# Lightning attention followed by a tanh-shrink MLP: causal scores and outputs in halves of 64 keys, and the attention pieces placed anew

## The chip, the cores and the metric

The kernel runs on one core of one Trainium2 chip. The metric is the device time of one execution in microseconds (us); lower is better. The engines are TensorE (PE; its weight loads are listed as PEld), VectorE (DVE), ScalarE (ACT), GpSimd (POOL) and SyncE (SP). SP and GpSimd issue most of the DMAs.

## What is computed

```python
def _attn_ref(q, k, v, lam):                 # 4 batches, 8 heads, 768 positions, 64 channels
    ...
    for b in range(nb):                      # blocks of 64 positions
        intra = np.einsum('bhic,bhjc->bhij', qb, kb) * Dmask[None]     # lam ** (i - j) for i >= j
        intra = np.einsum('bhij,bhjd->bhid', intra, vb)
        inter = np.einsum('bhid,bhde->bhie', qb * lam_pow[None], kv_state)
        out[:, :, sl] = intra + inter
        kv_state = lam_block[None, :, None, None] * kv_state + np.einsum('bhsd,bhse->bhde', kb * rev_pow, vb)

def _moe_ref(x, w_in, w_out):                # x: 3072 x 512, w_in: 512 x 2048, w_out: 2048 x 512
    h = x @ w_in
    return (h - np.tanh(h)) @ w_out
```

All data are float32 on the chip; the weights arrive as 64-bit floats and are rounded on the chip.

## The kernel before

The sequence is cut into 6 groups of 128 positions (`BLK`); a group with its 4 batches gives 512 token rows. One batch of one group is a *chunk* (g, b): 128 positions, 8 heads as 4 pairs p of 2 (j). Two chunks, (0, 1) or (2, 3), are a *half* of a group.

Dense part. Both matrix products use a Strassen-like scheme of seven products (A and B factors, `FACT`): `up` makes the hidden columns (line 458), tanh is taken on ScalarE (L466) and subtracted on VectorE, and `down`, `down_twice` and `inner_steps` (L640, L693, L542) make the output, some of them with a second level of seven products of 128x128 pieces. Weight pieces (`wb`, 256 KB) come from DRAM by GpSimd's DMA queue through a ring of seven buffers. Group 0 is worked otherwise: `up_plain` (L748) runs while the weights are still being rounded on ScalarE and VectorE (L289 to L296), and `down_first` (L778) while VectorE makes the factor sums (L787 among them).

Attention of group g + 1 runs inside the dense work of group g. For one half it has four pieces:

- `att_transpose` (L323): q and k with channels on partitions. For groups 0 and 1 by TensorE (L336), for later groups by loading 32x32 blocks (32 small DMAs for a chunk, on SP's queue, L143) and a VectorE transpose (L331). q times powers of lambda is made here as well (`qd`, L342).
- `att_scores` (L345): for each head a matmul with 64 rows (channels) by 128 keys, 128 queries moving; the two heads of a pair lie in different row halves of TensorE. VectorE multiplies the result by the decay mask (L356).
- `att_out` (L384): the state read (L400; 64x64 weights, four tiles of TensorE in turn), and the value product with all 128 keys (L406; 128x64 weights), both summed in two PSUM banks, which ScalarE copies to `xt` (L410).
- `att_state` (L363): k is multiplied by its decay (L361), the products of k and v (L374), then on VectorE the state times its decay (L379) plus the product (L380).

`attention(g)` returns these pieces, and the main loop (L887 to L939) places them by hand: the first half's transposes and scores after u = 2 and u = 3 of the up part, its output and state after the second down product; the second half's between the later ones. For group 1 the table `turns` (L846) does so. Each engine executes its own queue in order; the order of each queue is made from program order by a scheduler, except where `tied` or `keep_in_program_order` holds an operation to its place. PSUM has eight banks: `att` four, `ya`, `yb`, `z`, `w` one each.

SP's queue carries the loads of q, k, v (`load_natural`, L131: one DMA of 256 KB per chunk and tensor), the blocks (L143) and the input weights.

The functions that the change touches follow, with the line numbers of the profile.

Of the kernel before, what the change touches and what calls it, by code (L numbers as in the profile page):

```python
# [18 lines left out]
BLK = 128  # L19
# [5 lines left out]
def kernel(  # L25
# [69 lines left out]
    mask = const.tile([128, 2, NP, BLK], F32)  # L95
    for j in range(2):
        for p in range(NP):
            h = 2 * p + j
            nc.vector.tensor_tensor_scan(out=mask[:, j, p, :], data0=lam_all[:, h:h + 1].to_broadcast([128, BLK]),
                                         data1=ident, initial=0.0, op0=AL.mult, op1=AL.add)  # L100

# [13 lines left out]
    bwd = mask.rearrange("s j p i -> s p j i")[:, :, :, BLK - 1:BLK].to_broadcast([128, NP, 2, D])  # L115
# [11 lines left out]
    def load_natural(g, b, names):  # L127
        for name, src, bufs in (("q", q, 2), ("k", k, 3), ("v", v, 4)):
            if name in names:
                x = (qpool if name == "q" else io).tile([128, H, D], F32, name=f"{name}_nat", tag=name, bufs=bufs)  # L130
                op = nc.sync.dma_start(out=x, in_=src[b, :, ts(g, BLK), :].rearrange("h s d -> s h d"))  # L131
                tc.keep_in_program_order(op)
                raw[g, b][name] = x
# [189 lines left out]
    def att_transpose(g, bs):  # L323
        for b in bs:
# [4 lines left out]
            for dst, x in ((qt, "q"), (kt, "k")):  # L329
# [3 lines left out]
                else:  # L333
                    tp = bank("tp", "att", 4).rearrange("d (p s) -> d p s", p=NP)
                    for p in range(NP):
                        tied(g == 0 or p == 0, nc.tensor.transpose(out=tp[:, p, :], in_=t[x][:, 2 * p:2 * p + 2, :],  # L336
                                                                   identity=ident))
                    tied(g == 0, nc.scalar.activation(dst, tp, AF.Copy))
            qd = None
            if g > 0:  # L340
                qd = work.tile([128, NP, BLK], F32, name="qd", tag="qd")
                nc.vector.tensor_tensor(qd, qt, fwd, op=AL.mult)  # L342
            tr[g, b] = (qt, kt, qd)

    def att_scores(g, bs):  # L345
        for b in bs:
            qt, kt, _ = tr[g, b]

            sp = [bank("sp", "att", 4).rearrange("s (p i) -> s p i", p=NP) for _ in range(2)]
            for p in range(NP):  # L350
                for j in range(2):
                    tied(g == 0, nc.tensor.matmul(out=sp[j][:, p, :], lhsT=kt[ts(j, 64), p, :],  # L352
                                                  rhs=qt[ts(j, 64), p, :], start=True, stop=True))
            ss = work.tile([128, 2, NP, BLK], F32, name="ss", tag="ss")
            for j in range(2):
                tied(g == 0, nc.vector.tensor_tensor(ss[:, j], sp[j], mask[:, j], op=AL.mult))  # L356
            sc[g, b] = ss

    def att_decay(g, b):
        kp = raw[g, b]["k"].rearrange("s (p j) d -> s p j d", j=2)  # L360
        tied(g != 1, nc.vector.tensor_tensor(kp, kp, bwd, op=AL.mult))  # L361

    def att_state(g, bs):  # L363
        if g == NG - 1:
            return

        kv = bank("kv", "att", 4).rearrange("d (b p e) -> d b p e", b=2, p=NP)
        for n, b in enumerate(bs):
            kd, vn = raw[g, b]["k"], raw[g, b]["v"]
            if g > 0:  # L370
                att_decay(g, b)
            for p in range(NP):
                for j in range(2):
                    tied(g == 0, nc.tensor.matmul(out=kv[ts(j, 64), n, p, :], lhsT=kd[:, 2 * p + j, :],  # L374
                                                  rhs=vn[:, 2 * p + j, :], start=n == 0 and p == 0, stop=True,
                                                  skip_group_check=True))
        st = state[:, bs[0]:bs[0] + 2]
        if g > 0:
            nc.vector.tensor_tensor(st, st, lam_blk, op=AL.mult)  # L379
            nc.vector.tensor_tensor(st, st, kv, op=AL.add)  # L380
        else:
            tied(True, nc.scalar.activation(st, kv, AF.Copy))

    def att_out(g, bs):  # L384
        half = bs[0] // 2
# [584 lines left out]
```

## Time and profile before

| what | value |
|---|---|
| runs | 668.13, 667.68 and 666.55 us (median 667.68) |
| span of the profiled execution, the only time of its own that the page has | 665.0 us (the runs shown are 1.6 to 3.1 us longer) |
| TensorE busy | 653.9 us (98%) |
| VectorE busy | 480.1 us (72%) |
| ScalarE busy | 214.7 us (32%) |
| GpSimd busy | 195.8 us (29%) |
| moved | 121.74 MB, mean 183 GB/s |
| granted TensorE clock | 1.00 |

A line of a profile's order of time gives start, length (us), engine, source line, operation, out<-in, shapes and count; a bracket at its end gives the idle time of the engine ahead of it and what ended it. Successive instructions of one group are merged into one line. TensorE's matmuls overlap each other, so the distance between the starts of two groups says what the first one cost, and its listed length is a little longer. A float32 matmul of the program appears as two instructions.

### The profile page before, as it was taken

How to read it: one execution, taken by the hardware profiler on the slowest of the kernel's cores; microseconds unless marked ns; L12 is line 12 of the kernel's file. 1: busy time of each engine (PE TensorE's matmuls, PEld its weight loads, DVE VectorE, ACT ScalarE, POOL GpSimd, SP SyncE). 2: the span in 40 equal slices, each digit the busy share in tenths (PEclk: the TensorE clock that was granted, in tenths of full speed). 3: DMA queues.
4: the chain of work that ended last, by engine and by line, in shares of the span. 5: the costliest groups of instructions: out<-in, count | busy, mean ns of one | idle time of the engine just before them, and what ended most of it. 6: DMA issues, size and time to landing. Idle time of an engine off the chain costs nothing.

```text
span 665.0 us, 13269 instructions
## 1 busy us (share of the span) xinstructions
PE 653.9 (98%) x4992; PEld 594.7 (89%) x4992; DVE 480.1 (72%) x869; ACT 214.7 (32%) x413; POOL 195.8 (29%) x340
## 2 busy tenths in 40 slices
PE   8999999999999999999999999999999999999998
PEld 7788888888888999888999988999988899988897
DVE  4568898997778983579885379987368877357753
ACT  4778923423321112341112342112243112233110
POOL 0001416783112444001435101254301264400250
PEclk9999999999999999999999999999999999999999
DMA  9999936997345979425889543698731687610491
GB/s 216 231 205 263 300 123 215 352 316 219 81 93 145 303 221 276 80 35 135 226 247 277 146 74 73 165 286 255 216 72 38 186 260 258 222 37 1 116 295 64
DMA packets 158958, 121.74 MB, mean 183 GB/s; under 512 B 133872, under 2 KB 135024, under 8 KB 158896
## 3 DMA queue, kind: packets, MB, share of 16 engines
q0 software_dynamic: 26400, 86.27, 40.4%
q1 hardware_dynamic: 132352, 34.64, 25.3%
q8 instruction: 39, 0.64, 0.4%
q14 instruction: 23, 0.19, 0.1%
q10 hardware_dynamic: 144, 0.00, 0.0%
HBM read 100.67 MB, written 20.19 MB: 182 GB/s over the span
## 4 chain that ended last, share of the span: by engine, by line
PE 66%; issue 14%; DMA 8%; SPq 4%; POOL 3%; DVE 3%; ACT 1%; POOLq 0%; DVEq 0%; ACTq 0%
PE y L458 13%; PE y L693 12%; PE zw L693 9%; PE z L458 8%; PE y L542 4%; PE w L640 4%; PE y L640 4%; PE sp L352 2%; PE z L542 2%; DMA raw<-in_moe_w_in_dram 2%; PE h L748 2%; DMA wb<-fine 2%; PE op L406 2%; SPq L131 2%; SPq L143 1%
## 5 line engine op out<-in xcount | busy, mean ns | idle before, releaser
L605 POOL DMA_DIRECT2D wb<-fine x168 | 90.5, 539 | 170.3 <-PE y L693 55.9
L466 ACT ACTIVATE th<-g 128x512 f32<-128x512 f32 x76 | 47.6, 630 | 99.5 <-DVE g L471 34.2
L696 ACT ACTIVATE q<-y 128x128 f32<-128x128 f32 x96 | 26.6, 277 | 149.6 <-PE y L693 148.6
L458 PE MATMUL y<-xt,w 128*128 128x256 f32 x320 | 73.5, 380 | 0.0
L458 PEld LDWEIGHTS y<-xt,w 128*128 128x128 f32 x320 | 59.9, 190 | 8.5 <-ACT g L546 0.9
L467 DVE TENSOR_TENSOR g<-g,th 128x512 f32<-128x512 f32 x76 | 52.1, 689 | 21.1 <-ACT th L466 21.0
L693 PE MATMUL y<-wb,g 128*128 128x128 f32 x456 | 60.6, 278 | 0.0
L748 PE MATMUL h<-xt,w 128*128 128x256 f32 x256 | 58.0, 383 | 2.0 <-DVE w L296 2.0
L748 PEld LDWEIGHTS h<-xt,w 128*128 128x128 f32 x256 | 47.7, 190 | 9.9 <-DVE w L296 2.7
L693 PEld LDWEIGHTS y<-wb,g 128*128 128x128 f32 x456 | 55.1, 192 | 1.3 <-issue 0.3
L608 POOL DMA_DIRECT2D wb<-factors x44 | 23.8, 541 | 96.0 <-PE y L640 64.6
L693 PE MATMUL zw<-wb,g 128*128 128x128 f32 x304 | 40.3, 275 | 0.1
L458 PE MATMUL z<-tt,ws 128*128 128x256 f32 x160 | 38.1, 381 | 0.0
L458 PE MATMUL y<-tt,ws 128*128 128x256 f32 x160 | 37.8, 379 | 0.0
L458 PE MATMUL z<-xt,ws 128*128 128x256 f32 x160 | 37.8, 379 | 0.0
L693 PEld LDWEIGHTS zw<-wb,g 128*128 128x128 f32 x304 | 37.0, 192 | 0.2 <-DVE g L698 0.2
L640 PE MATMUL w<-wb,g 128*128 128x256 f32 x160 | 35.8, 382 | 0.0
L640 PE MATMUL y<-wb,g 128*128 128x256 f32 x160 | 35.3, 379 | 0.0
L356 DVE TENSOR_TENSOR ss<-sp,mask 128x512 f32<-128x512 f32 x48 | 31.1, 684 | 5.8 <-PE sp L352 5.8
L640 PEld LDWEIGHTS y<-wb,g 128*128 128x128 f32 x160 | 30.4, 190 | 4.1
L458 PEld LDWEIGHTS z<-xt,ws 128*128 128x128 f32 x160 | 30.4, 190 | 4.1
L640 PEld LDWEIGHTS w<-wb,g 128*128 128x128 f32 x160 | 30.1, 190 | 4.4
(178 smaller groups left out, 1292.6 us busy)
## 6 DMA issues: line engine op xcount, KB each, us to landing
wb<-fine POOLq DMA_DIRECT2D x168, 256.0 KB, 4.2
wb<-factors POOLq DMA_DIRECT2D x44, 256.0 KB, 4.5
v_nat<-in_v_dram SPq DMA_DIRECT2D x24, 256.0 KB, 5.2
wb<-fine_in POOLq DMA_DIRECT2D x24, 256.0 KB, 4.3
k_nat<-in_k_dram SPq DMA_DIRECT2D x20, 256.0 KB, 5.0
raw<-in_moe_w_out_dram POOLq DMA_DIRECT2D x10, 512.0 KB, 4.9
raw<-in_moe_w_in_dram SPq DMA_DIRECT2D x8, 512.0 KB, 6.0
raw<-in_moe_w_in_dram SPq DMA_DIRECT2D x16, 256.0 KB, 5.6
```

The lines of the kernel that those rows point to most:

```text
L131: op = nc.sync.dma_start(out=x, in_=src[b, :, ts(g, BLK), :].rearrange("h s d -> s h d"))
L356: tied(g == 0, nc.vector.tensor_tensor(ss[:, j], sp[j], mask[:, j], op=AL.mult))
L458: nc.tensor.matmul(out=t[:, m, :], lhsT=wt[:, kt, ts(m, 128)], rhs=x[:, kt, :], start=first and m == 0 and kt == 0, stop=kt == 1, skip_gro ...
L466: nc.scalar.activation(th, src, AF.Tanh)
L467: nc.vector.tensor_tensor(dst(c), src, th, op=AL.subtract)
L542: nc.tensor.matmul(out=dst[:, ts(u, 128)], lhsT=a, rhs=b, start=x in (1, 2, 5) and u == 0, stop=True, skip_group_check=True)
L605: nc.gpsimd.dma_start(out=t.rearrange("p m c -> p (m c)"), in_=fine[TWICE.index(n_), SUB.index(x_)].rearrange("p u c -> p (u c)"))
L608: nc.gpsimd.dma_start(out=t, in_=factors[XAT[FACT[n_][1]]][:, 2 * x_:2 * x_ + 2, :])
L640: nc.tensor.matmul(out=t[:, m, :], lhsT=a[:, u, kt, ts(m, 128)], rhs=wb[:, kt, :], start=first and u == 0 and m == 0 and kt == 0, stop=u = ...
L693: nc.tensor.matmul(out=dst, lhsT=a[:, u, :], rhs=wb[:, ts(u, 128)], start=x in (1, 2) and u == 0, stop=u == NU - 1, skip_group_check=True)
L696: nc.scalar.activation(keep, dst, AF.Copy)
L748: tied(u == 0, nc.tensor.matmul(out=hm[c][:, m, :], lhsT=w1[u][:, i, a, ts(m, 128)], rhs=xt[0, t][:, i, :], start=m == 0 and i == 0, stop= ...
```

## The change

From group 1 on, causality is used in halves of 64 keys (`HF`). Early keys (the first 64 of a chunk) are scored against all 128 queries, late keys only against the last 64. For the upper two pairs the two key halves change places on the partitions, so that four 64x64 tiles of TensorE are in use in turn. Masks are 384 wide for each j and chunk instead of 512. The value product becomes `out_late` (128x64 weights: for the last 64 queries all keys) and `out_early` (64x64 weights: for the first 64 queries the early keys).

- k and v of groups from 1 on are loaded by three DMAs each (128, 64 and 64 rows) instead of one, and k has four buffers instead of three.
- The mask of group 0 lies in the buffer `tt`; `masks()` builds the new one from it with four scans on VectorE and small copies on GpSimd.
- The decay of a chunk's k is two operations of 256 columns, called ahead of the stretch, and `qd` has a call of its own.
- `att_stretch` runs state read, state products, state update and late output; then, where `nxt` is given, the scores of the other half; then the early output. Without `nxt` the first matmul of `out_early` gets a wait on the state's add. With `nxt` the scores also use the banks `ya`, `yb` and `w`, and the state product has the bank `ya` or `yb`.
- Matmuls of attention are all held in program order.
- `pieces` places them anew: in group 2 both halves' stretches stay apart from scores; in groups 1, 3 and 4 the first half's stretch takes in the second half's scores; transposes of groups 4 and 5 start at the end of the dense work of the group before; group 5 has read, late and early output at separate places.

```diff
-    mask = const.tile([128, 2, NP, BLK], F32)
+    HF = BLK // 2
+    mask0 = xpool.tile([128, 3, 2, HB], F32, name="tt", tag="tt").rearrange(
+        "s a b c -> s (a b c)")[:, 0:2 * NP * BLK].rearrange("s (j p i) -> s j p i", j=2, p=NP)
...
+    mask = const.tile([128, 4, 3, HF], F32)
+    def masks():
...
+        for n in range(4):
+            tc.keep_in_program_order(nc.vector.tensor_tensor_scan(
+                out=cross[hi, n].rearrange("s c i -> s (c i)"), data0=lam_all[hi, n + 4:n + 5].to_broadcast([HF, BLK]),
+                data1=inj[hi], initial=0.0, op0=AL.mult, op1=AL.add))
...
-        for name, src, bufs in (("q", q, 2), ("k", k, 3), ("v", v, 4)):
+        for name, src, bufs in (("q", q, 2), ("k", k, 4), ("v", v, 4)):
...
+                    for rows, hs, at_ in ((slice(0, BLK), 0, 0), (slice(0, HF), NP, HF), (slice(HF, BLK), NP, 0)):
+                        n = rows.stop - rows.start
+                        part = src[b, hs:hs + NP, g * BLK + at_:g * BLK + at_ + n, :]
+                        tc.keep_in_program_order(nc.sync.dma_start(out=x[rows, hs:hs + NP], in_=part.rearrange("h s d -> s h d")))
...
+    def score_products(g, b, tags):
+        qt, kt, _ = tr[g, b]
+        sp = [bank("sp", t, 4 if t == "att" else 1)[:, 0:6 * HF].rearrange("s (q c i) -> s q c i", q=2, c=3) for t in tags]
...
+        for late_, rows, cols in ((False, slice(0, BLK), lambda c: slice(0, 1 + c, c)), (True, slice(HF, BLK), None)):
+            for q in range(2):
+                for j in range(2):
+                    for p in (q, q + 2):
+                        c = 1 + p // 2
+                        dst = sp[j][half(p, late_), q, c if late_ else cols(c), :]
+                        tied(True, nc.tensor.matmul(out=dst, lhsT=keys(p, j, late_), rhs=qt[ts(j, 64), p, rows],
+                                                    start=True, stop=True))
...
+    def out_late(g, bs):
...
+                    tied(True, nc.tensor.matmul(out=dst(n, p, j)[:, HF:BLK], lhsT=vn[:, 2 * p + j, :],
+                                                rhs=ss[:, j, p % 2, 1 + p // 2, :], start=False, stop=True,
+                                                skip_group_check=True))
+    def out_early(g, bs, behind=None):
...
+                        r = ts(p // 2, HF)
+                        mm = tied(True, nc.tensor.matmul(out=dst(n, p, j)[:, 0:HF], lhsT=vn[r, 2 * p + j, :],
+                                                         rhs=ss[r, j, q, 0, :], start=False, stop=True,
+                                                         skip_group_check=True))
+                        if behind is not None:
+                            tc.add_manual_dep(mm.ins, behind.ins.name, mybir.DependencyInfo(
+                                mybir.DependencyClass.Sync, mybir.DependencyReason.DATA), reason="state read")
+                            behind = None
+        copy_xt(g, bs[0] // 2, ops)
+    def att_stretch(g, bs, nxt=None, kvtag="att", tags=()):
+        att_read(g, bs)
+        kv = state_products(g, bs, bank("kv", kvtag, 4 if kvtag == "att" else 1))
+        st = state[:, bs[0]:bs[0] + 2]
+        nc.vector.tensor_tensor(st, st, lam_blk, op=AL.mult)
+        add = nc.vector.tensor_tensor(st, st, kv, op=AL.add)
+        out_late(g, bs)
+        if nxt is not None:
+            sp = [score_products(g, b, tags[2 * n:2 * n + 2]) for n, b in enumerate(nxt)]
+        out_early(g, bs, None if nxt is not None else add)
...
-    turns = [(1, 11, 1, ()), (1, 21, 1, ()), (1, 12, 1, ()), (1, 22, 1, ()), (2, 11, 2, p0[0:1]), (2, 21, 2, p0[1:2]),
-             (3, 11, 1, ()), (3, 21, 1, p0[2:4]), (2, 12, 1, ()), (2, 22, 1, p1[0:1]), (3, 12, 1, p1[1:2]),
-             (3, 22, 1, ())]
+    turns = [(1, 11, 1, ()), (1, 21, 1, ()), (1, 12, 1, ()), (1, 22, 1, ()),
+             (2, 11, 2, ((att_transpose, 1, P0), (att_qd, 1, P0))), (2, 21, 2, ((att_scores, 1, P0), (att_decay, 1, P0))),
+             (3, 11, 1, ((att_transpose, 1, (2,)),)),
+             (3, 21, 1, ((att_transpose, 1, (3,)), (att_stretch, 1, P0, P1, "ya", ("att", "att", "yb", "ya")), (att_qd, 1, P1))),
+             (2, 12, 1, ()), (2, 22, 1, ((att_decay, 1, P1),)), (3, 12, 1, ()), (3, 22, 1, ())]
...
+    def pieces(g, at_):
+        h, k = g + 1, g + 2
+        if g == 1:
+            table = {2: [(att_transpose, h, P0)], 3: [(att_scores, h, P0), (att_qd, h, P0), (att_decay, h, P0)],
+                     "P2": [(att_stretch, h, P0)], "P4": [(att_transpose, h, P1)],
+                     "P5": [(att_scores, h, P1), (att_qd, h, P1), (att_decay, h, P1)],
+                     "P6": [(att_stretch, h, P1), (att_sums, h)]}
+        elif g == 2:
+            table = {0: [(att_transpose, h, P0)], 1: [(att_scores, h, P0), (att_qd, h, P0)], 2: [(att_transpose, h, (2,))],
+                     3: [(att_transpose, h, (3,)), (att_decay, h, P0)]}
+        else:
+            table = {1: [(att_transpose, h, P1)], 3: [(att_decay, h, P0)] if h < NG - 1 else []}
+        if 1 < g < NG - 2:
+            table.update({"P2": [(att_stretch, h, P0, P1, "yb", ("att", "att", "w", "yb")), (att_qd, h, P1)],
+                          "P5": [(att_decay, h, P1)], "P6": [(att_stretch, h, P1), (att_sums, h)],
+                          "inner": [(att_transpose, k, P0)], "end": [(att_scores, k, P0), (att_qd, k, P0)]})
+        if g == NG - 2:
+            table.update({"P2": [(att_read, h, P0), (att_scores, h, P1, ("att", "att", "w", "yb"))],
+                          "P4": [(out_late, h, P0), (out_early, h, P0), (att_qd, h, P1)], "P5": [(att_read, h, P1)],
+                          "P6": [(out_late, h, P1), (out_early, h, P1), (att_sums, h)]})
+        run(table.get(at_, ()) if g < NG - 1 else ())
```

In `pieces`, the numbers are the steps u of the up part of group g, and P2 to P6 the places after down products 2, 4, 5 and 6.

## The prediction

> **What bounds the kernel now.** I read the page first, then the clock, TensorE's order of time round one attention stretch, the single instruction starts in it, and VectorE's order of time at the same place.
>
> ```profile
> span 665.0 us, 13269 instructions
> ...
> PE 653.9 (98%) x4992; PEld 594.7 (89%) x4992; DVE 480.1 (72%) x869; ACT 214.7 (32%) x413; POOL 195.8 (29%) x340
> ...
> PEclk9999999999999999999999999999999999999999
> ```
>
> TensorE is busy 98% of the span at full clock. So the time follows the work and the waits on TensorE, and little else. Attention from the second group on is what the change touches; here is one half of group 2 (two chunks), in TensorE's order of time (start, length, line, shapes):
>
> ```profile
> 202.49 2.06 PE L352 MATMUL sp<-qt,kt 64*128 64x128 f32 x32
> 204.47 7.17 PE L640 MATMUL w<-wb,g 128*128 128x256 f32 x32
> 211.57 1.10 PE L400 MATMUL op<-qd,state 64*64 64x128 f32 x32
> 212.61 1.97 PE L406 MATMUL op<-ss,v_nat 128*64 128x128 f32 x32
> 214.41 1.10 PE L374 MATMUL kv<-v_nat,k_nat 128*64 128x64 f32 x32
> 215.44 1.16 PE L693 MATMUL y<-wb,g 128*128 128x128 f32 x8
> ```
>
> Read the starts, not the lengths: scores 1.98 us, read 1.04, output 1.80, state 1.03, then dense work again. With 0.09 at each entry a half costs 2.08 + 3.95 = 6.03 us; the five groups repeat it within 0.01. (A float32 product stands as two instructions.)
>
> **Prices, from single starts in these stretches.** The read puts four 64x64 tiles side by side: starts at 0, 6, 13 and 20 ns, and the next four 109 ns after (128 columns). Scores and output have two tiles side by side, also 109 to 112 ns. The state has two tiles of 64 columns every 58.5 ns. First weights of a mode: 0.05 us for 64 columns. Changing the tile shape: 0.11 (read's last group to output: 0.22 for a slot of 0.11). Back to dense: 0.10 drain, plus 0.10 of dense weights not loaded ahead.
>
> **Unknown price:** four 64x64 tiles with 64 columns. Bounds: 58.5 ns a group (state row) and 109 (read row, as if halving bought nothing). I take 58.5: in the read, the second set of four weight loads starts 55 ns after the first, so four loads side by side keep up with it.
>
> **The matmuls, per half.** Scores become 8 groups of 128 columns (early keys) and 8 of 64 (late): 0.09 + 0.05 + 0.87 + 0.47 + 0.10 = 1.58 us alone, 0.50 less than 2.08. Output becomes 16 pairs of 64 columns (0.94, state row) plus 8 groups (0.47), but with one more change of shape. A stretch of read, state, late, early: 0.09 + 0.92 + 0.11 + 0.99 + 0.94 + 0.16 + 0.47 + 0.10 = 3.77, 0.18 less than 3.95. Merged with the other half's scores (1.34): 5.12 against 6.03, and one dense return less: 1.02 saved.
>
> By the built order of the changed kernel, groups 1, 3 and 4 have one stretch of each kind: 0.50 + 1.02 + 0.18 = 1.69 each. Group 2 keeps its four apart: 1.35. The last (no state; 2 x 5.10 before) runs five pieces, 1.58, 2.45, 1.81, 1.11 and 1.81, with one more return: 1.34. Rows alone: **-7.8 us**.
>
> **What comes back as waits.** The early output of an unmerged stretch now waits for the state add on VectorE; in a merged one the last scores reuse the bank that the add empties. VectorE is in order, and what stands ahead of the add decides. Group 2's first half, before:
>
> ```profile
> 213.47 0.68 DVE L664 TENSOR_TENSOR o<-q,w 128x512 f32<-128x512 f32 x1
> ...
> 215.27 0.68 DVE L379 TENSOR_TENSOR state<-state,fwd 128x512 f32<-128x512 f32 x1
> ...
> 218.28 0.68 DVE L380 TENSOR_TENSOR state<-state,kv 128x512 f32<-128x512 f32 x1
> ```
>
> The add ended 3.5 us after dense work had resumed, and nobody cared. It starts a new piece every 0.60 us there. In the new order I walk from 204.65, the start of the first mask: four masks of 384 elements (0.47 each, about three quarters of 0.60), two sums of 0.60 and eight small ones of 0.20 bring it to 209.4; nine pieces of 0.60, the o above among them, to 214.8; then the state's product, one more sum and the add (0.65, 0.60, 0.70): end at 216.7. The read starts at 211.05 (scores saved 0.5) and the early output could start 3.07 later, at 214.1. **Wait 2.6 us.** Queued behind it on TensorE: all the down product.
>
> At the second half of groups 2, 3 and 4 the five pieces that close the sixth product stand ahead:
>
> ```profile
> 238.84 0.69 DVE L707 TENSOR_TENSOR q<-q,q 128x512 f32<-128x512 f32 x1
> 239.57 1.29 DVE L709 TENSOR_TENSOR q<-q,q 128x512 f32<-128x512 f32 x2
> 240.78 0.69 DVE L379 TENSOR_TENSOR state<-state,fwd 128x512 f32<-128x512 f32 x1
> ```
>
> With the decays gone from before them they start 0.3 earlier; product and add end at 241.9; the early output could start at 238.16 + 3.07 = 241.2. 0.7 each, 2.1 together. The merged stretches of groups 3 and 4: the new order puts the add's end 4.45 us after the read's start, the bank is wanted at 3.8: 0.65 each, 1.3. Sum of these six pieces of waiting: **+6.0**.
>
> **Group 1** runs while weights are still rounded: ScalarE busy 13.3 and VectorE 13.0 of the 14 us from 58 to 72. Two new add waits (about 1.8 and 1.0 by the same walk) stand against filling a weight wait of 0.9 to 1.1 at 67.2 with transposes and dense work moved ahead; later the first down product already waits for VectorE (0.6 and 0.2 on L787). I let 0.5 of its 1.7 survive: **+1.2**. The split loads also fall here: eight more DMAs on SP ahead of weights. Between 0 (SP is already held back by full queues: v took 2.84 where q took 0.58) and 8 x 0.58 = 4.6 us; value 0.
>
> **What goes away:** TensorE waits of 0.3 and 0.9 at 223 to 225, 0.9 at 333 and some 0.6 more from 425 to 545, most of them on wb pieces landing. TensorE arrives later at the first, and the blocks for groups 4 and 5 load earlier, away from the down products. I take 1.5 of 2.7: **-1.5**. Ends: none, and all.
>
> **At nothing:** four scans of 64x128 (0.40 each by L99) and nine small GpSimd pieces at about 36 us, where VectorE is busy 17.3 of 28 us and GpSimd idle until 57; uncovered 1.6 and some 3 us (0.2 to 0.3 each by the identity's rows). Two decays of 256 cost 0.12 more than one of 512, two masks save 0.27. Transposes put earlier: SP then must deliver group 3's first blocks by about 272; from the release at 213 it takes 6 us of natural loads and four blocks of 8 us, 253; if that cover went, VectorE and all behind it would stand. Later SP waits 31 and 29 us for buffers, so its extra 0.5 us issues are covered.
>
> **Sum:** -7.8 + 6.0 + 1.2 - 1.5 = -2.1. On the profiled 665.0 us that is 662.9; the runs shown lie 1.6 to 3.1 above the span (median 667.68), so I forecast **665.6 us**.
>
> **Rivals.**
> - *The waits stay hidden* (0.13). For: part of the work ahead of the add could slip behind it. Against: the new order has it in front. Then -7.8 + 1.2 of group 1 and, as TensorE comes no later to the wb pieces, only 0.6 of relief: -7.2, 660.5.
> - *The saving is only exchanged for waits* (0.15): VectorE, 77.6 of 105 us busy per group, sets each down product's pace, and TensorE's gain returns to it. Only the 0.5 of group 1 stays: 667.2. It is also the case in which halving the keys does not do what it says.
> - *The add comes later still* (0.22), the one on the other side. Place: the eight waits (two each in groups 1 to 4). Price: each 0.1 us of lateness beyond my walk costs 0.8. From 0.26 each the gain is gone; at one more 128x512 piece each (0.60 x 8 = 4.8) the time is 670.4. For it: any VectorE piece that itself waits adds up; against: the walk used measured starts.
> - *Half-width groups cost a full one* (0.09): 160 groups x 50.5 ns = 8.1 us, 673.7; pays back the gain from 71.6 ns a group on. Against: the 55 ns above.
>
> The Trainium skill's "TensorE: Matmul & The Clock Gate", Back-to-back issue gap, gives matmuls of 1 to 64 columns a floor of about 25 ns start to start, so 100 ns for a group of four; by it the last rival's price would be an estimated 6.6 us and the time about 672. The trace speaks against it: tiles side by side start 6 to 7 ns apart. It has 0.03 of that rival's 0.09.
>
> **How the numbers follow.** Forecast case 0.41, its own spread 663 to 668. About 0.2%, 1.3 us, is what a measurement here can tell from no change. The forecast case splits into 0.33 faster, 0.07 same, 0.01 slower; the exchange for waits into 0.01, 0.13, 0.01. Faster: 0.33 + 0.13 + 0.01 = 0.47. Same: 0.07 + 0.13 = 0.20. Slower: 0.01 + 0.01 + 0.22 + 0.09 = 0.33. Range **660.5 to 671.5**: it takes in the first three cases and all but the far end of the add's lateness, and leaves out the half-width rival and a full 4.6 us on SP.
>
> **What would show it.** Right: scores of a half end 1.5 us after their start; state's 32 instructions still 0.94; groups of 64 columns every 58 to 60 ns; TensorE idle before the early output "<-DVE state", 2 to 3 us at the first half of group 2 and 0.5 to 1 at the others; fewer waits on wb. Wrong: groups of 64 columns at 100 ns; no idle there; waits on q_blk or k_blk by VectorE; weights landing later than 53 us in group 1's stage.

## The result, and the profile after

The changed kernel takes 673.91 us (median of 4 runs, 672.60 to 676.93); the kernel before, run beside it, 667.24 us. The ratio is **1.0112, 95% interval 1.008 to 1.0144**: about 1% slower. The forecast was 665.6 us, the range 660.5 to 671.5; a loss had been given a chance of 0.33.

The page of the changed kernel, its span, TensorE's share and clock:

```profile
span 670.3 us, 14720 instructions
...
PE 647.2 (97%) x5632; PEld 588.6 (88%) x5632; DVE 477.3 (71%) x889; ACT 214.5 (32%) x413; POOL 200.8 (30%) x349
...
PEclk9999999999999999999999999999999999999999
```

TensorE's busy time fell by 6.7 us (the rows had forecast 7.8), and the span grew by 5.3: TensorE now stands still for 23 us where it stood for 11. Its waits name what for (engine, line, what it waited for: us in all, times, longest):

```profile
PE op L502 <- DVE state L517: 5.7, 5, 2.5
PE y L800 <- DMA wb<-fine: 2.7, 4, 1.3
...
PE sp L451 <- DVE state L517: 2.2, 3, 1.2
...
PE zw L800 <- DVE ss L458: 1.4, 1, 1.4
```

L502 is the early output, L451 the scores, L517 the state's add, L800 the down products, L458 the masks. The first and third lines are the waits that the forecast had. The other two it had not. The first half of group 2 in TensorE's order, to be read beside the same stretch of before:

```profile
203.15 1.57 PE L451 MATMUL sp<-qt,kt 64*64 64x128 f32 x64
204.65 7.17 PE L747 MATMUL w<-wb,g 128*128 128x256 f32 x32
211.75 1.10 PE L481 MATMUL op<-qd,state 64*64 64x128 f32 x32
212.79 1.15 PE L414 MATMUL kv<-v_nat,k_nat 128*64 128x64 f32 x32
213.77 1.10 PE L490 MATMUL op<-ss,v_nat 128*64 128x64 f32 x32
217.37 0.69 PE L502 MATMUL op<-ss,v_nat 64*64 64x64 f32 x32 [2.49 <-DVE state L517]
```

Scores end 1.50 us after their start, early output takes 0.62; between late and early output lies the wait (bracket: idle time, and what ended it). VectorE at that place, with the o, the state's product and the add that the prediction named:

```profile
213.60 0.68 DVE L771 TENSOR_TENSOR o<-q,w 128x512 f32<-128x512 f32 x1
...
215.43 0.69 DVE L516 TENSOR_TENSOR state<-state,fwd 128x512 f32<-128x512 f32 x1
...
216.63 0.68 DVE L517 TENSOR_TENSOR state<-state,kv 128x512 f32<-128x512 f32 x1
```

VectorE never stops here, and the add simply stands late in its queue: it ends at 217.3, TensorE goes on at 217.37.

**Where the time came from.** I take the start of the same dense product in both traces and follow by how much the changed kernel lags. It lags 0.2 us at 204 us (0.7 without what group 2's first scores save), 2.6 behind group 2's first stretch, 4.2 behind its second, 3.8 where the down products that hold group 3's attention begin, 3.9 at those of group 4, 4.8 at those of group 5, 5.3 at the end. The pieces of TensorE's order, with their waits taken off, give the rows.

| term | forecast | measured | out of |
|---|---|---|---|
| rows, groups 2 to 5 | -6.1 | -5.8 | half scores 1.59 for 2.08; stretch 3.77 for 3.95; merged 5.21 for 6.03; last group behind its first scores 7.19 for 8.12 |
| waits for the add, groups 2 to 4 | +6.0 | +6.7 | 2.56 + 3 x 0.84 + 2 x 0.81 |
| group 1 in all | -0.5 | +0.7 | lag at 204 us |
| masks of the last group | 0 | +1.4 | L458 wait at 545 us |
| wb pieces and all else | -1.5 | +2.3 | what is left of 5.3 |
| sum | -2.1 | +5.3 | spans 665.0 and 670.3 |

The forecast misses the span by 5.3 + 2.1 = 7.4 us: 0.3 on rows, 0.7 on the add's waits, 1.2 in group 1, 1.4 for the masks, 3.8 in the row of wb pieces and all else. Of that row's +2.3, the waits for wb pieces that can be named make +1.6 (at 222 to 240 us 2.8 for 1.4 before; 0.6 at 368 and 0.5 at 443 are new; 0.9 at 333 is gone); the other 0.7 is not placed.

And the profiled execution is one of the better ones: two of the four took 675.2 and 676.9. The median lies 3.6 us above the profiled span, where the forecast had added 2.7. The clock, below, is a part of this.

### The profile page after: what moved, and what is told of

Its sections match the earlier page's. It is cut to its first block, busy times and chain, and to the rows that moved or that the text cites. A ratio compares the mean times of both kernels' runs of the same rounds, so it can differ in the third digit from the quotient of the medians.

```text
span 670.3 us, 14720 instructions
## 1 busy us (share of the span) xinstructions
PE 647.2 (97%) x5632; PEld 588.6 (88%) x5632; DVE 477.3 (71%) x889; ACT 214.5 (32%) x413; POOL 200.8 (30%) x349
## 4 chain that ended last, share of the span: by engine, by line
PE 51%; SPq 19%; DMA 12%; DVE 8%; issue 4%; ACT 4%; POOL 1%; DVEq 0%; ACTq 0%; POOLq 0%
SPq L174 14%; PE y L800 8%; PE acc L889 7%; DMA q_blk<-in_q_dram 6%; PE h L859 6%; PE y L565 6%; PE zw L800 6%; PE z L565 4%; PE w L747 3%; PE y L747 3%; PE y L649 3%; DMA v_nat<-in_v_dram 3%; SPq L163 2%; SPq L158 2%; DVE g L574 2%
## 5 line engine op out<-in xcount | busy, mean ns | idle before, releaser
L800 PE MATMUL y<-wb,g 128*128 128x128 f32 x456 | 60.6, 278 | 1.8 <-DMA wb<-fine 1.8
L800 PEld LDWEIGHTS y<-wb,g 128*128 128x128 f32 x456 | 55.1, 192 | 3.0 <-issue 2.3
L800 PE MATMUL zw<-wb,g 128*128 128x128 f32 x304 | 40.2, 275 | 0.0
L800 PEld LDWEIGHTS zw<-wb,g 128*128 128x128 f32 x304 | 37.0, 192 | 0.0
L565 PEld LDWEIGHTS z<-tt,ws 128*128 128x128 f32 x160 | 29.5, 190 | 5.6 <-DVE g L601 1.8
```

Source lines behind the costliest of these rows:

```text
L565: nc.tensor.matmul(out=t[:, m, :], lhsT=wt[:, kt, ts(m, 128)], rhs=x[:, kt, :], start=first and m == 0 and kt == 0, stop=kt == 1, skip_gro ...
L800: nc.tensor.matmul(out=dst, lhsT=a[:, u, :], rhs=wb[:, ts(u, 128)], start=x in (1, 2) and u == 0, stop=u == NU - 1, skip_group_check=True)
```

## The experiments

All ratios are to the kernel before, run beside the experiment on the same chip. The experiments ran on four chips (e1 to e4, e5 to e8, e9 to e12, e13 and e14), so across these sets the ratios are the better comparison.

| kernel | median us | ratio (95% interval) |
|---|---|---|
| changed | 673.91 | 1.0112 (1.008 to 1.0144) |
| e1_peek | 677.80 | 1.0165 (1.0144 to 1.0186) |
| e2_free_bank | 676.18 | 1.0132 (1.0096 to 1.0168) |
| e3_whole_loads | 679.75 | 1.0186 (1.0161 to 1.0212) |
| e4_old_order | 670.42 | 1.0047 (1.0028 to 1.0066) |
| e5_early_peek | 673.34 | 1.0092 (1.0062 to 1.0121) |
| e6_all | 671.09 | 1.0083 (1.0053 to 1.0114) |
| e7_spread | 674.97 | 1.0124 (1.0104 to 1.0143) |
| e8_from_third | 664.46 | 0.9957 (0.9934 to 0.998) |
| e9_third_spread | 662.40 | 0.992 (0.990 to 0.9939) |
| e10_all_third_spread | 666.60 | 0.9985 (0.9964 to 1.0007) |
| e11_group1 | 674.05 | 1.0099 (1.0075 to 1.0124) |
| e12_keep_busy | 677.79 | 1.0158 (1.0123 to 1.0194) |
| e13_late_transpose | 663.00 | 0.9925 (0.9903 to 0.9948) |
| e14_before_spread | 666.09 | 0.9988 (0.9971 to 1.0004) |

My first theory: the waits for the add are the loss, and what is taken off them comes back, but for a part that wb pieces take. Rival: TensorE's time is only exchanged between waits.

### The add's wait: e1, e2, e5

Read and early output write the same bank from different row halves of TensorE, and the program puts a wait between them. In every kernel with halves here one lies between them (in merged stretches by way of the last scores), so no run shows what happens without it; the add is only what the wait hangs on. So another, cheaper operation to wait for was tried: a copy of one element on ScalarE (`peek`).

```diff
+        look = work.tile([128, 1], F32, name="look", tag="look")
+        peek = nc.scalar.activation(look, kv[:, 0:1, 0, 0], AF.Copy)   # e1, e2: behind the add; e5: ahead of the state's two operations
-        out_early(g, bs, None if nxt is not None else add)
+        out_early(g, bs, None if nxt is not None else peek)            # e1; e5 from group 2 on
+        out_early(g, bs, peek if nxt is not None else add)             # e2
```

> The changed kernel, but in the six stretches that are not merged the first early-output product waits for a one-element copy on ScalarE (it reads the state product's bank) and no longer for the state add on VectorE. Theory (the add waits are real losses of TensorE): the gaps between late and early output, 2.6 us in group 2's first half, 0.8 in the second halves of groups 2 to 4 and 1.0 in group 1, together 6.0 us, shrink to below 0.2 each; wb pieces that land late take up to half of it back, so 668 to 671 against 673.9. Rival (the time is only exchanged: TensorE arrives earlier and waits for wb or VectorE instead): gaps gone, time 673 to 674. Second rival (ScalarE is late itself): gaps stay over 0.5.

e1's edit missed its aim. The copy was written behind the add, reads the same bank, and so waited for the add itself; the gap before the early output was 2.75 us. e2 (state product in bank z, in group 1 in w; the same copy, for the merged stretches) missed in the same way:

> The changed kernel, but the three merged stretches put the state product into a bank of its own (z; in group 1 w) that no score product of the stretch reuses; the early output waits for a one-element copy on ScalarE. Theory: the waits of the last scores for the state add (0.8 us each in groups 3 and 4, 1.2 in group 1) go; 2.9 us less, at least 1.5 of it kept: 671.0 to 672.4. Rival (exchange): 673 to 674.

The waits at the merged stretches of groups 3 and 4 only fell from 0.81 to 0.40, now ahead of the early output. In group 1 a gap of 3.2 us appeared ahead of the last transposes; the trace puts it down to a load of k that landed late, not to the copy. Neither run tells theory and rival apart. What they show is the price of a long gap (below).

> The changed kernel, but in the unmerged stretches of groups 2 to 4 the first early-output product waits for a one-element copy on ScalarE that stands ahead of the state's product and add and so needs the state products alone (in e1_peek the copy came out behind the add, and the wait stayed). Theory (the add waits are real losses): the gaps before the early output in groups 2 to 4 (2.6, 0.8, 0.8, 0.8 us) fall below 0.3, the half-speed stretch of the clock that follows the 2.6 us gap in most executions does not come, wb pieces take up to 2.6 back: 667.5 to 670.5 against 673.9. Rival (exchange for wb waits): 672.5 to 674.

In e5 the copy waits for TensorE alone. TensorE's order there:

```profile
215.39 1.10 PE L490 MATMUL op<-ss,v_nat 128*64 128x64 f32 x32
216.42 0.69 PE L502 MATMUL op<-ss,v_nat 64*64 64x64 f32 x32
```

The wait is gone, and at groups 3 and 4's second halves too. But the median is 673.34, the theory's 667.5 to 670.5 missed: of 5.1 us of waits removed, 0.6 came back by the medians (by the ratios 1.3, within the intervals). The rival's time came out, and the trace says through what. Gaps of 1.0 (a difference on VectorE), 0.6 (wb) and 1.8 us (no releaser in the trace, "issue") now stand at 229 to 246 us, and one of 2.1 at 369 for a wb piece; half-speed clock follows the last. By the lag to the changed kernel, the profiled execution of e5 had lost 1.5 us by 134 us, ahead of every place that the edit touches; it then gained 2.8 by 351 us, and at 369 it lost 3.0. So the removed waits did come through for a while, and not all that was lost was lost in exchange for them.

### Wb pieces beside k and v: e3, e7

At 222 to 246 us SyncE issues k and v of three chunks in a row (18 transfers, 223.7 to 244.8), where before it issued two in 215 to 219 and the third at 242. The third chunk's k, before and after (start, time to issue, count):

```profile
241.70 0.37 SPq L131 DMA_DIRECT2D k_nat<-in_k_dram  x1
```

```profile
233.38 7.26 SPq L163 DMA_DIRECT2D k_nat<-in_k_dram  x3
```

Before, SyncE stood for 18.3 us ahead of it, waiting for VectorE's decay of an earlier k to be done with a buffer; now k has a fourth buffer, and no wait of SyncE in this stretch is over 1.8. The first two chunks also come some 9 us later than before. No run here gives k its three buffers back, so the shares of the two are not known. In the window of 222 to 246 us the wb pieces take from issue to landing (last column, median us) before, after and in e9:

```profile
wb<-fine POOLq DMA_DIRECT2D x19, 256.0 KB, 4.3
```

```profile
wb<-fine POOLq DMA_DIRECT2D x18, 256.0 KB, 6.5
```

```profile
wb<-fine POOLq DMA_DIRECT2D x19, 256.0 KB, 4.8
```

A down product uses a piece in 0.89 us and seven buffers hold pieces: by this estimate 7 x 0.89 = 6.2 us are covered, 6.5 are not.

```diff
-                if name == "q" or g == 0:                      # e3: k and v of all groups as one transfer
+                if True:
-            first = {GB: (0, 1, 2), GB + 1: (0, 1)}.get(g, ()) # e7: group 3's first k, v behind the blocks of chunk 1
+            first = {GB: (0, 1, 2)}.get(g, ())
...
```

> The changed kernel, but k and v of groups 1 to 5 are loaded with one transfer each as before, not with three (heads 4 to 7 then hold their two key halves in the wrong rows; the work is the same). Two causes are possible for the new waits of TensorE for wb pieces at 230 to 239 us (2.8 us) and later (1.1 us). Theory A: three chunks' k and v come in one burst beside the down products, since k has a fourth buffer; bytes and moment stay, so the waits stay within 1 us of 2.8 and the time is 673 to 674.5. Theory B: the many small transfers themselves slow the wb pieces; the waits fall to 1.4 (their size before) or less and the time to 670 to 672.

e3 leaves out the change of places of the two key halves that masks and outputs count on, so it does the same work on other rows. Its time (679.75) fits neither theory and is inconclusive: its group 1 came out in another order, with gaps of 1.6 and 2.0 us, group 2's first stretch had one of 3.3, and three intervals of half-speed clock came with them. At the place in question (224 to 248 us) wb pieces landed in 6.2 us, hardly sooner than with split loads, and gaps of 1.1 and 0.4 remained. That the number of transfers is the cause finds little support.

> The changed kernel, but SyncE issues k and v of group 3's first two chunks behind the blocks of these chunks, so some 30 us later, in place of ahead of all of group 3's blocks. Theory A (new wb waits at 230 to 239 us come from three chunks' k and v loaded beside the down products): these waits fall from 2.8 us to 1.2 or less, 671.5 to 672.5. Theory B (not the burst): they stay, 673 to 674.5.

In e7 the gaps on wb pieces there are 0.6 and 0.6, together 1.3 for 2.8, and a piece lands in 5.0 us: theory A's mechanism. Its time did not follow (674.97). In the profiled execution two things took the 1.6 us back: half clock at 219 us (1.7) and new gaps at 339 to 341 us (1.2 together, the longer one for a wb piece). For the median this is not shown: three of the changed kernel's four executions have a lowered clock too.

### The clock: e7, e12, and the other traces

TensorE in e7, by stretches of 3.4 us (length, TensorE's busy time and instructions, granted clock, share of the DMA engines, GB/s):

```profile
215.40:218.80 3.40, 1.33 (x38) 1.00 0.38 103
218.80:222.20 3.40, 3.40 (x19) 0.50 0.33 91
222.20:225.60 3.40, 3.40 (x32) 1.00 0.73 193
```

The wait for the add left TensorE idle for some 2.1 us of the first stretch, and **for the next 3.41 us it had half its clock**: by estimate 1.7 us of work lost on top of the wait. Apart from drops that begin behind the last products, the drops in all traces last 3.41 us or twice that, and within a trace they lie on one grid of time. Laying this grid over TensorE's busy time, the eleven intervals ahead of a drop have 1.8 to 2.7 us of idle time (e1, e2 twice, e3 twice, e4, e5, e6, e7, e10 and e12). Three intervals with 1.87 to 1.93 us had no drop behind them (changed kernel, e11, e14), and no other has more than 1.64. In e3 and e6 a drop went on for a second interval, with 1.2 and 1.0 us idle in its first. So the bound is near 1.8 to 1.9 us, and it isn't sharp in these records. The profiled execution of the changed kernel is one of the three; its wait of 2.6 us runs over the end of the interval, 0.6 of it into the next (after the length: TensorE, its weight loads, VectorE, ScalarE, GpSimd, clock, DMA share, GB/s):

```profile
213.40:216.80 3.40, 1.47 (x52) 1.33 (x46) 3.40 (x7) 0.00 (x0) 0.72 (x1) 1.00 0.79 192
216.80:220.20 3.40, 2.83 (x51) 2.77 (x52) 1.83 (x4) 1.36 (x3) 0.56 (x1) 1.00 0.38 102
```

One half-speed interval in 670 us makes a mean clock of 0.997. Three of four executions of the changed kernel show that (one of them took no more than the profiled one, 672.6, so it is not the whole of the spread), and of the 56 executions of before beside the experiments, 3 do. In e10 the twelve executions sort by it: the five at 1.00 have a median of 664.84 us, the five at 0.997 one of 667.88, and the two at 0.995 took 669.17 and 670.07. That is more than 1.7 us for a drop; the wait that brings it comes on top. The Trainium skill, "TensorE: Matmul & The Clock Gate", What's actually happening, names a free-running window of 3413 ns for this; the traces agree, their single drops last 3.413 us. The Trainium skill's advice in Why this matters for your kernels is to have no idle gaps over about 3 us; here 1.8 to 2.7 us within one interval were enough, and the measurement decides.

> The changed kernel with ten products of the 128x128 identity into the unused bank z (2.3 us of work that no output needs) between late and early output of group 2's first half, that is inside the 2.6 us wait. Theory (TensorE idle for 2.0 us or more of one 3.41 us interval gets half the clock in the next one, 1.7 us lost): the early output starts at the same time, and no interval at half clock follows in any execution; mean clock 1.00 in all and 672 to 673, against 673.9. Rival (the half clock has another cause): 0.997 in about half of the executions as before, and 674 or more.

```diff
         out_late(g, bs)
+        if g == 2 and bs == (0, 1):
+            warm = bank("idle", "z", 1)
+            for _ in range(10):
+                tied(True, nc.tensor.matmul(out=warm[:, 0:128], lhsT=ident, rhs=ident, start=True, stop=True))
```

```profile
215.32 2.50 PE L522 MATMUL idle<-ident 128*128 128x128 f32 x20
217.97 0.69 PE L502 MATMUL op<-ss,v_nat 64*64 64x64 f32 x32 [0.15 <-DVE state L517]
```

At this place e12 did as expected: the early output starts 3.7 us after the late one as in the changed kernel (3.6), and no half clock follows. "In all executions" failed: four of six show 0.997 or less. In the profiled one a drop comes later, at 249.0, behind a wait of 0.8 for the add and 1.8 us of idle time for which the trace shows no releaser ("issue"). That no drop follows at the filled place agrees with the theory but does not test it, since the profiled execution of the changed kernel has none there either. The theory rests on the eleven intervals above. The time missed its forecast (677.79 for 672 to 673): the profiled execution lost 1.8 us at that gap and 1.5 by the drop behind it, but even the two executions at 1.00 took 674.2 and 676.3, and that is not explained.

### Halves alone, in the old places: e4, e8, e9, e14

e4 keeps scores, masks and loads of halves, in the order of before (read, late, early, state), with the copy on ScalarE.

```diff
-            table = {2: ... "P2": [(att_stretch, h, P0)] ...}   # only g == 1
+            # the same table for every group; att_stretch: read, copy, late, early, state; no merged stretch
```

> Halves of 64 keys alone: scores, masks, loads and outputs of the changed kernel, but in the places of the kernel before (transposes, scores, then read, late and early output, then state; no merged stretch), the early output behind a one-element copy on ScalarE. Theory (halving the keys pays by rows, the new placement loses): scores save 0.49 us in each of 10 halves and a stretch about 0.05 in each; 5.0 to 5.5 us by rows, so 661.5 to 663.5. Rival (the loads or the masks that the halves need cost what the rows save): 666 to 669. Second rival (time is only exchanged for wb waits): 665.5 to 667.

670.42: missed, and by the trace for one reason. In group 1 ScalarE rounds weights, and the copy queued behind that:

```profile
80.92 1.48 PE L490 MATMUL op<-ss,v_nat 128*64 128x64 f32 x24 [2.74 <-ACT look L516]
```

Half clock followed at 81.0 to 84.4. By the lag to before, e4 had lost 5.4 us at 204 us; from the down products that hold group 3's attention on it gained 3.4 us. So e8 and e9 leave group 1 as before, and e9 moves the loads too:

> Halves of 64 keys from group 2 on, in the places of the kernel before and with the copy on ScalarE ahead of the early output; group 1 is computed with whole keys, loads and places of the kernel before. In e4_old_order, group 1 alone lost 5.5 us (the copy queued on ScalarE behind weight rounding, then the half-speed clock), and groups 3 to 5 won 3.9. Theory (halving pays by rows wherever no wait is added): -0.49 for each of 8 score halves and -0.05 for each stretch, 4.3 us less, of which wb waits in group 2 take up to 2: 662.5 to 665. Rival (loads and masks cost what the rows save): 666.5 to 669.

> e8_from_third with group 3's first k and v issued later, as in e7_spread. Theory (what is left of new waits in group 2 are wb pieces beside the burst): the waits of 0.4, 0.8 and 0.6 us at 228 to 245 us shrink by 1 us together: 0.9957 becomes about 0.994 of before. Rival: the burst is only moved on to other wb pieces: 0.9955 to 0.998.

Both theories came true, e9 by more than expected. It is **0.8% faster than the kernel before** and, on another chip, 1.7% faster than the change (662.40 to 673.91; by the ratios 1.9%). Its page:

```profile
span 659.2 us, 14410 instructions
...
PE 649.7 (99%) x5504; PEld 590.4 (90%) x5504; DVE 476.8 (72%) x885; ACT 215.8 (33%) x421; POOL 199.7 (30%) x349
```

TensorE is busy for 2.5 us longer than in the changed kernel, and the span is 11.1 us shorter. Its stretches of groups 2 to 4 take 4.03 us against 3.95 before, those of the last group 2.95 against 3.02; so all that halving saves by rows is in the scores, 8 x 0.49 = 3.9, less 0.3 for the stretches.

> The kernel before with nothing changed but the issue place of group 3's first k and v (whole transfers, behind the blocks of these chunks). It tells how much of e9_third_spread's 0.8% is the loads' place and not the halves. Theory: before waits 1.4 us for wb pieces at 220 to 226 us beside such loads; at most this comes back: 0.998 to 1.000 of before, so that halves are worth at least 0.6%. Rival (most of the gain is the loads' place): 0.995 or less.

The loads' place alone gives before 0.9988, at most 0.3%; e9's span is 5.1 us below e14's. The rows give 3.6 of it; waits of 0.6 and 0.7 us at 227 and 332 us, which e14 has and e9 has not, give 1.3. The halves with all that came along in e9 are worth some 0.7%.

### The new placement without its waits: e6, e10, e13, e11

> As e5_early_peek, and in groups 3 and 4 the state product of the merged stretch has the bank z, which no score of the stretch needs (0.8 us each), and the last group's first half runs read, late output, scores of the other two chunks and early output in one stretch, so that VectorE's masks no longer wait for an early output two products later (1.5 us). Theory: 3.2 us below e5_early_peek, 664.5 to 667.5. Rival (exchange for wb waits): within 1 us of e5_early_peek.

e6 (e5, the merged product in z, and the last group's first half in one stretch):

```diff
-            table.update({"P2": [(att_read, h, P0), (att_scores, h, P1, ("att", "att", "w", "yb"))],
-                          "P4": [(out_late, h, P0), (out_early, h, P0), (att_qd, h, P1)], ...
+            table.update({"P2": [(last_stretch, h, P0, P1, ("att", "att", "w", "yb"))], "P4": [(att_qd, h, P1)], ...
```

671.09 is 3.6 us above the theory's upper bound. It is 2.3 below e5, more than the rival allows, but five executions of each spread over 5 to 6 us and the intervals of the ratios overlap, so that this difference is not clear of the noise. The waits in the merged stretches and the masks' wait went; these two lines of the changed kernel show that last one, TensorE first, then VectorE (its masks wait for the early output, which frees their buffer, and the bank that holds the scores is the one the next down product writes):

```profile
545.38 0.94 PE L800 MATMUL zw<-wb,gS 128*128 128x128 f32 x6 [1.38 <-DVE ss L458]
```

```profile
543.84 1.95 DVE L458 TENSOR_TENSOR ss<-sp,mask 128x384 f32<-128x384 f32 x4 [1.45 <-PE op L502]
```

In their place the profiled execution of e6 has one gap of 3.8 us that ends at 230.6 and two intervals of half clock. VectorE stood in front of a transpose:

```profile
229.20 0.71 DVE L362 STREAM_TRANSPOSE kt<-k_blk 128x512 f32<-128x512 f32 x1 [4.04 <-DMA k_blk<-in_k_dram]
```

A difference that the next down product needs stands behind it. e10 adds e8's group 1 and e7's loads; its edit is the sum of these.

> The new placement with its waits taken out (e6_all), group 1 computed with whole keys in the places of before, and the loads as in e7_spread. Theory (the new placement is worth no more than the old one once its waits are gone; in both, groups 3 to 5 won 4.0 us): the same ratio to before as e9_third_spread within 0.3%. Rival (merged stretches save 1 us each by rows and it counts): 2 us or more below e9_third_spread.

e10 came out 4 us above e9 on the same chip: the theory that both are alike failed, and the rival too. Three lines of e10, VectorE, GpSimd, TensorE:

```profile
357.78 0.71 DVE L366 STREAM_TRANSPOSE kt<-k_blk 128x512 f32<-128x512 f32 x1 [4.12 <-DMA q_blk<-in_q_dram]
```

```profile
359.63 0.72 POOL L787 DMA_DIRECT2D out_dram<-q  x1 [4.41 <-ACT r L718]
```

```profile
365.56 1.13 PE L863 MATMUL y<-wb,g 128*128 128x128 f32 x8 [3.44 <-DMA wb<-fine]
```

To be read as a chain: the new placement puts the next group's transposes amid the inner product. The transpose waits 4.1 us for its blocks; behind it on VectorE stands the closing of product 7 (it starts at 358.4); behind that, on GpSimd, the store of its result (the trace puts this wait down to ScalarE, but by the program the store waits for that closing sum, and in e10, e5 and the changed kernel alike it starts some 0.6 us behind the sum's end); behind the store the issue of the next wb piece at 360.35; and TensorE needs it at 362. The changed kernel has the same chain at 361 to 369, with 1.5 us at its head and 0.6 at its end; e5 has 2.4 and 2.1. Its head in the changed kernel:

```profile
361.43 0.71 DVE L362 STREAM_TRANSPOSE kt<-k_blk 128x512 f32<-128x512 f32 x1 [1.51 <-DMA q_blk<-in_q_dram]
```

e13 takes only the transposes away from there:

```diff
...
-                          "inner": [(att_transpose, k, P0)], "end": [(att_scores, k, P0), (att_qd, k, P0)]})
+                          "end": [(att_transpose, k, P0), (att_scores, k, P0), (att_qd, k, P0)]})
```

> e10_all_third_spread, but the next group's first transposes stand directly ahead of their scores, as late as they can, and no longer amid the inner product. Theory (in e10 VectorE's transposes wait 4.1 us for q and k blocks; behind them stands the closing of product 7, behind its store on GpSimd the issue of the next wb piece, and TensorE waits 3.4 us for it and then runs at half clock): this chain goes in groups 2 and 3, the time falls by 3 to 5 us from 666.6, to the level of e9_third_spread (662.4) or up to 1.5 below. Rival (the placement loses elsewhere): 665 or more.

663.00: with the transposes moved the time falls by 3.6 us, as expected, and the chain is gone from this place in the trace. No execution of e13 shows a lower clock; set against e10's five at 1.00 (664.84), about half of the 3.6 goes with the drops. So the new placement comes level with the old one with halves (0.9925 and 0.992). It is not yet free of waits. At its new place a transpose still waits for its blocks:

```profile
398.27 0.71 DVE L366 STREAM_TRANSPOSE kt<-k_blk 128x512 f32<-128x512 f32 x1 [2.13 <-DMA k_blk<-in_k_dram]
```

Behind it TensorE waits 0.9 and 1.3 us for VectorE at 399 to 403 us, and 0.6 at 507; e9 has no such wait. Whether merged stretches would gain something without these waits, no run shows.

> The changed kernel, but group 1 is computed with whole keys, loads and places of the kernel before. Theory: in the changed kernel group 1 lost 0.7 us where its rows alone would have won 1.7; its removal gives 0.7 to 1.5 back: 672.4 to 673.2, and the other waits stay as they are (2.6, three of 0.8, 2.8 for wb, 1.5 in the last group). Rival (group 1's placement brings a gain): 674.5 or more.

e11 (group 1 whole, the rest as changed): 674.05, so neither side of the expectation. By the lag it gained 0.7 us at 204 us, as the theory said, and lost them again at 226 to 249 us, mostly to wb pieces: gaps of 1.5, 0.7, 0.3, 0.7 and 0.5 (the last without a releaser).

## Why the prediction was wrong, step by step

**Rows: right.** Half scores 1.59 (forecast 1.58), unmerged stretch 3.77 (3.77), merged 5.21 (5.12). Groups of four with 64 columns start 58 ns apart. The half-width rival, and the floor of 25 ns that the Trainium skill gives (TensorE: Matmul & The Clock Gate, Back-to-back issue gap), are out for tiles side by side. The rival's 673.7 is the number of the prediction that comes nearest to 673.91; since its mechanism is out, that is a coincidence.

**The waits for the add: right in place and size.** 2.56 us for 2.6, 0.84 for 0.7, 0.81 for 0.65. So the rival that the add comes later still did not happen either: the sign came out on its side through other causes.

**"What goes away: -1.5": failed, and its sign with it.** The step read the buffer of k only as freedom for the loads. It lets a third chunk's k and v run beside the down products that hold group 2's attention; wb pieces land in 6.5 us where by estimate 6.2 are covered, and TensorE's gaps there grew from 1.4 to 2.8 us. Before's 0.9 us at 333 did go, but 0.6 at 368 and 0.5 at 443 came. e7 moves two chunks' loads alone, and the gaps there fall to 1.3; e9 does the same to e8, and the ratio goes from 0.9957 to 0.992. That the fourth buffer brought the third chunk there rests on SyncE's waits, not on a run.

**"At nothing: transposes put earlier": failed.** The cover was worked out for group 3's first blocks at 272 us; the transposes amid the inner product of the next group were not checked, and there SyncE's blocks are 1.5 us late in the changed kernel, 2.4 in e5 and 4.1 in e10, which reach the place sooner. The prediction's own sign, VectorE waiting on q_blk or k_blk, appeared. In the changed kernel it costs TensorE 0.6 us; e10 against e13 shows the price where other waits are gone: 3.6 us.

**The last group's -1.34: half right.** Its rows were; a wait of 1.4 us for masks, whose buffer the postponed early output holds, was not seen. e6 took it away.

**Group 1: the term was mis-sized by 1.2 us.** The waits for the add were 1.2 and 1.0 (forecast 1.8 and 1.0), but the weights' wait was not filled: 0.4 and 1.0 at 68 and 70 us remain, and gaps of 0.7 at 64 to 65 us are new, part of them for the transposed k that ScalarE copies.

**Not in the sum at all: the clock.** A wait of 2.6 us was priced at 2.6. Where enough of it falls into one interval of the clock, as in e1, e2 and e7, it costs by estimate 1.7 more.

**"The saving is only exchanged for waits" was the rival nearest in kind**, though its 667.2 stopped at an even exchange, and it named VectorE's work as what sets the pace. What took the gain was waits for wb pieces, blocks, masks and the add, and the clock; e9, with VectorE busy for 476.8 us where before has 480.1, keeps its gain. e5 and e11 showed some exchange at work; e9 and e13 showed that it is not a law: it ends when the loads and the transposes are moved.

What stays open: 0.7 us of the changed kernel's loss, e12's time, the 1.8 us of "issue" in it, and why e3's group 1 lost as much as it did. For the gaps of "issue" there is a candidate: ahead of those in e4 (1.1 us at 249 us), e5 and e12 a 16 KB packet of the queue that the page lists as q8, instruction, ended 1.4 to 1.6 us before TensorE went on, so instructions that came late are possible. Such packets also stand where no gap follows (changed kernel, e9), and no run tests it.

## What to carry to other kernels

Ask of every new buffer and every earlier load what it will now run beside: a transfer that was held back by a missing buffer was also held away from the stage that needs the DMA engines. Where an in-order engine gets an instruction earlier, take the latest of its inputs and follow every queue behind it, down to the stores that stand ahead of the next loads. And a saving by rows is kept by the plainest placement that has no new wait: halves with the old order beat the change by 1.7%, and the new placement, freed of its largest waits, came level with them and not below.

## What was not expected of the hardware

Idle time of 1.8 us or more within one 3.41 us interval was followed by half of TensorE's clock for the whole next interval in eleven cases of fourteen, in kernels that otherwise hold 1.00: by estimate 1.7 us per event. The traces suggest that it depends on how a wait falls on the interval's bounds (the changed kernel's 2.6 us wait was split into 1.9 and 0.6 and had no drop behind it), and executions of one kernel differ by it (e10: medians of 664.84 and 667.88 us without and with one drop). A wait for one semaphore was seen put down to a neighbour that ended at about the same time (ScalarE for VectorE at GpSimd's store), and only the order of the program and of the queues told which it was.
